# Attention with packed queries and a gated FFN on one core: the second batch's P run scored with the first units, its weights turned through DRAM, and the steps listed anew

## The chip, the cores and the metric

The kernel runs on one core of a Trainium2 chip. The metric is device time in microseconds (us). The core has TensorE (PE for its matmuls, PEld for its weight loads), VectorE (DVE), ScalarE (ACT), GpSimd (POOL) and SyncE (SP), which here issues nearly all DMA transfers. Each engine has its own queue and works through it in order.

## The reference

Eight batches of eight heads, 576 tokens, head dimension 64. Thirty-two packed queries P attend to the tokens of their batch and head, then the tokens attend to what the packed queries gathered, and a gated feed-forward net runs over all 4608 tokens:

```
def sm_attn(qq, kk, vv):
    s = scale * np.matmul(qq, kk.transpose(0, 1, 3, 2))
    s = s - np.max(s, axis=-1, keepdims=True)
    a = np.exp(s)
    a = a / (np.sum(a, axis=-1, keepdims=True) + 1e-09)
    return np.matmul(a, vv)
p_packed = sm_attn(p, k, v)              # (8, 8, 32, 64)
out = sm_attn(q, p_packed, p_packed)     # (8, 8, 576, 64)
x = out.transpose(0, 2, 1, 3).reshape(4608, 512)
h = x @ w_in                             # w_in 512 x 2048
g = h * (1.0 / (1.0 + np.exp(-1.702 * h)))
result = g @ w_out                       # w_out 2048 x 512
```

All inputs and the output are float32.

## The kernel before

The work is done batch by batch, with the attention of the next batch woven into the FFN of the present one. The heads of a batch are held as two groups, eo = 0 and 1, of four heads with 32 packed queries each: 128 partitions.

**The P run of a batch.** `scores1_mm` (L278, its matmuls in L250) multiplies P with the keys, a half (288 tokens) at a time and both groups together, into two PSUM banks. `scores1_copy` (L289) copies a bank into an SBUF tile x of 576 columns; `scores1_max` (L293, the reduction is L295) takes the maximum of one bank, so that there are four per batch; `bias1` (L299) joins the two maxima of a group and scales them. `exp1` (L317) makes the weights. These must be turned, since the tokens are the contraction of the next product. There are two ways to do it. By TensorE: `turn1_mm` (L339, matmul L343, four transposes into a bank), `turn1_copy` (L345), and for the last 64 tokens `turn1_last_mm` (L351, matmul L354) and `turn1_last_copy` (L358), which puts them into the tile aT. By VectorE and DRAM: `turn1_blocks` (L372, L374) transposes every 32x32 block of a group, eight `turn1_out` (L376, L382) per batch write the blocks to the DRAM tile aside, and six `turn1_in` (L384, L394) read them in another order into aT. Batches 0 and 1 go by TensorE, batches 2 to 7 by DRAM. `pack` (L396, matmul L406) multiplies with v; `pack_end` and the `pack_turn` steps make PT, the transposed packed values.

**The token run.** `scores2_mm` (matmul L493) multiplies q with PT, `scores2_turn` (L504) is a block transpose by DVE out of PSUM, `max2` (L524), `sub2` (L528), `exp2` (L532), `sum2` (L537 to L539) and `norm2` (L543) are the softmax, `turn2` (L549) turns back. `a_upper` and `a_lower` split its result into two parts ahi and alo of lower precision, whose sum is the value.

**The FFN.** `m_chunk` (L435) multiplies PT with a 512-wide part of w_in, so the attention's second product and the first FFN product become one: `h_mm` (matmul L603) is six matmuls of 288 columns from the split halves. A step `m_chunk b, fc` makes the factors of four units of h (a unit is 128 of the 2048 columns), and `m_upper` and `m_lower` (L469) split them. `h_tanh` (L611) and `h_gate` (L593) are the gate, `h_upper` (through `move`, L117 on ACT and L119 on DVE) and `h_lower` (L590) split g into ghi and glo, and `out_mm` is three matmuls of 512 columns (L663) that add a unit to one of four token tiles in PSUM. `store` (L682) writes a finished token tile. What a batch has beyond four token tiles of 128 is collected in over tiles.

**The FFN weights** come in as 64-bit words. `load_w n` (L189) loads one of 32 pieces, `begin_w` (L208, ACT) and `join_w` (L220, DVE) make float32 of it, and for w_out `upper_w` (a `move`) and `lower_w` (L232, POOL unless told otherwise) split it. Weights 4 to 7, 12 to 15, 20 to 23 and 28 to 31 are the four rows of w_out pieces that the units 0 to 15 of out_mm need, all in batch 0, where they arrive just ahead of use; the others are w_in.

**What sets the order.** A tuple `order` in the kernel (L707 to L1399) lists 2860 steps, and a loop (L1400) runs them. An instruction is put on its engine's queue where its step stands in the list. In `order`, `inner` names the two banks of h_mm (psh), `bank_b` the two banks used by m_chunk and pack (psb), `early` and `late` the four banks of out_mm. The x tiles have five buffers; a step that needs a new one waits for the oldest to be read. An engine's name at the end of a step (`dve`, `pool`) says where it runs.

Of the kernel before, what the change touches and what calls it, by code (L numbers as in the profile page):

```python
# [8 lines left out]
F32 = mybir.dt.float32  # L9
# [6 lines left out]
ALU = mybir.AluOpType  # L16
AX = mybir.AxisListType
# [4 lines left out]
def kernel(  # L22
# [77 lines left out]
    def x_tile(name):  # L100
        return wk.tile([P, S], F32, tag="x", name=name, bufs=5)
# [191 lines left out]
    def scores1_max(b, half, eo):  # L293
        bank = st["bank", 1, b, half][eo]
        nc.vector.tensor_reduce(  # L295
            st["mx", 1, b, eo][:, half : half + 1], bank[:, :NH], axis=AX.X, op=ALU.max
        )
# [399 lines left out]
    def over_store(pair, k, engine=nc.sync):  # L697
# [10 lines left out]
        (load, "k", 0, 0), (scores1_first, 0), (load, "k", 0, 1), (max1_first, 1, 0),  # L708
        (max1_first, 0, 0), (scores1_first, 1), (warm, 7, 3), (max1_first, 0, 1), (bias1, 0, 0),
        (exp1_first, 0, 0), (exp1_first, 0, 1), (turn1_mm, 0, 0), (max1_first, 1, 1),  # L710
        (bias1, 0, 1), (exp1_first, 1, 0), (exp1_first, 1, 1), (load_w, 1, 0), (sum1, 0, 0),
        (warm, 4, 2), (load, "v", 0, 0), (turn1_copy, 0, 0, dve), (turn1_mm, 0, 1),
        (turn1_last_mm, 0), (sum1, 0, 1), (load, "v", 0, 1), (turn1_last_copy, 0, dve),
        (pack, 0, 0, late), (turn1_copy, 0, 1), (pack, 0, 1), (begin_w, 1, 0), (join_w, 1, 0),
        (pack_end, 0), (load_w, 2, 0), (begin_w, 2, 0), (warm, 5, 2), (join_w, 2, 0),
        (pack_turn_mm, 0), (pack_turn_copy, 0), (load, "q", 0, 0), (scores2_mm, 0, 0),
        (scores2_turn, 0, 0, 0), (max2, 0, 0, 0), (scores2_turn, 0, 0, 1), (max2, 0, 0, 1),
        (sub2, 0, 0, 0, pool), (warm, 0, 3), (load_w, 3, 0), (begin_w, 3, 0), (warm, 8, 3),
        (warm, 9, 3), (load_w, 0, 0), (begin_w, 0, 0), (join_w, 3, 0), (exp2, 0, 0, 0),
        (join_w, 0, 0), (sum2, 0, 0, 0), (norm2, 0, 0, 0, pool), (load, "q", 0, 1),  # L720
        (scores2_mm, 0, 1, late), (scores2_turn, 0, 1, 0), (scores2_turn, 0, 1, 1), (max2, 0, 1),
        (load_w, 3, 1), (warm, 10, 3), (load_w, 4), (begin_w, 3, 1), (join_w, 3, 1),
        (m_chunk, 0, 0, early, 0), (turn2, 0, 0, 0), (m_upper, 0, 0, 0, 0), (m_upper, 0, 0, 1, 0),
        (sub2, 0, 0, 1, pool), (warm, 6, 2), (exp2, 0, 0, 1), (sum2, 0, 0, 1), (begin_w, 4),
        (join_w, 4), (a_upper, 0, 0, 0), (a_lower_mm, 0, 0, 0, bank_b), (sub2, 0, 1, None, pool),
        (exp2, 0, 1), (upper_w, 4), (a_lower_copy, 0, 0, 0), (load_w, 1, 1), (begin_w, 1, 1),
        (warm, 3, 3), (load_w, 0, 1), (sum2, 0, 1), (begin_w, 0, 1), (norm2, 0, 0, 1, pool),
        (turn2, 0, 0, 1), (load_w, 2, 1), (a_upper, 0, 0, 1), (m_lower, 0, 0, 0, 0), (warm, 2, 3),
        (begin_w, 2, 1), (m_lower, 0, 0, 1, 0), (join_w, 1, 1), (a_lower_mm, 0, 0, 1, bank_b),
        (a_lower_copy, 0, 0, 1), (h_mm, 0, 0, 0), (norm2, 0, 1, None, pool), (turn2, 0, 1),  # L730
        (lower_w, 4), (h_mm, 0, 1, 0), (h_tanh, 0, 0, 0), (a_upper, 0, 1, None), (a_lower, 0, 1),
        (h_tanh, 0, 1, 0), (join_w, 0, 1), (load_w, 5), (begin_w, 5), (join_w, 2, 1),
        (m_chunk, 0, 0, (bank_b, bank_b), 1), (load_w, 7), (begin_w, 7), (h_gate, 0, 0, 0),
        (h_upper, 0, 0, 0), (m_upper, 0, 0, 1, 1, dve), (h_mm, 0, 0, 1), (h_gate, 0, 1, 0),
        (h_upper, 0, 1, 0), (join_w, 5), (m_lower, 0, 0, 1, 1), (h_tanh, 0, 0, 1), (h_over, 0, 0),
        (h_gate, 0, 0, 1), (h_upper, 0, 0, 1, dve), (h_lower, 0, 0, 1, dve), (load_w, 6),
        (h_lower, 0, 0, 0), (h_mm, 0, 1, 1), (out_mm, 0, 0, 0), (upper_w, 5),
        (m_upper, 0, 0, 0, 1), (m_lower, 0, 0, 0, 1), (h_tanh, 0, 1, 1), (h_gate, 0, 1, 1),
        (out_mm, 0, 0, 1), (h_over, 0, 1), (out_mm, 0, 0, 3), (begin_w, 6), (join_w, 6),
        (load_w, 8), (begin_w, 8), (join_w, 8), (h_lower, 0, 1, 0), (h_mm, 0, 2, 1),  # L740
        (h_tanh, 0, 2, 1), (h_over, 0, 2), (load_w, 9), (lower_w, 5), (out_mm, 0, 1, 0),
        (h_upper, 0, 1, 1), (begin_w, 9), (load_w, 10), (begin_w, 10), (h_mm, 0, 2, 0),
        (h_tanh, 0, 2, 0), (join_w, 7), (join_w, 9), (out_mm, 0, 0, 2), (h_lower, 0, 1, 1),
        (out_mm, 0, 1, 3), (out_mm, 0, 1, 2), (load_w, 11), (h_gate, 0, 2, 1), (h_gate, 0, 2, 0),
        (begin_w, 11), (join_w, 11), (out_mm, 0, 1, 1), (upper_w, 6), (join_w, 10),
        (load, "k", 1, 0), (scores1_mm, 1, 0, inner), (load, "k", 1, 1), (scores1_max, 1, 0, 0),
        (h_upper, 0, 2, 0), (h_upper, 0, 2, 1), (h_lower, 0, 2, 0, dve), (scores1_copy, 1, 0, 0),
        (upper_w, 7), (scores1_max, 1, 0, 1), (m_chunk, 0, 1), (m_upper, 0, 1, 0, None, dve),
        (scores1_copy, 1, 0, 1), (load_w, 12), (begin_w, 12), (h_lower, 0, 2, 1), (h_mm, 0, 3, 0),
        (h_tanh, 0, 3, 0), (lower_w, 6), (h_mm, 0, 3, 1), (m_lower, 0, 1, 0), (out_mm, 0, 2, 2),  # L750
        (m_upper, 0, 1, 1, None), (h_gate, 0, 3, 0), (join_w, 12), (out_mm, 0, 2, 1), (lower_w, 7),
        (m_lower, 0, 1, 1), (h_upper, 0, 3, 0), (upper_w, 12), (lower_w, 12), (out_mm, 0, 2, 3),
        (load_w, 18), (h_lower, 0, 3, 0), (h_tanh, 0, 3, 1), (h_gate, 0, 3, 1), (h_over, 0, 3),
        (h_mm, 0, 4, 0), (h_tanh, 0, 4, 0), (h_gate, 0, 4, 0), (h_upper, 0, 4, 0),
        (h_upper, 0, 3, 1), (h_lower, 0, 3, 1), (out_mm, 0, 2, 0), (h_mm, 0, 4, 1),
        (h_tanh, 0, 4, 1), (out_mm, 0, 3, 0), (h_over, 0, 4), (h_gate, 0, 4, 1),
        (h_upper, 0, 4, 1, dve), (h_lower, 0, 4, 1, dve), (h_mm, 0, 5, 1), (load_w, 13),
        (begin_w, 13), (join_w, 13), (load_w, 14), (begin_w, 14), (join_w, 14), (out_mm, 0, 3, 2),
        (h_tanh, 0, 5, 1), (h_mm, 0, 5, 0), (h_over, 0, 5), (h_gate, 0, 5, 1), (h_lower, 0, 4, 0),
        (out_mm, 0, 4, 0), (out_mm, 0, 3, 1), (load_w, 15), (begin_w, 15), (upper_w, 13),  # L760
        (lower_w, 13), (h_tanh, 0, 5, 0), (h_gate, 0, 5, 0), (load_w, 17), (begin_w, 17),
        (join_w, 17), (h_upper, 0, 5, 0), (out_mm, 0, 4, 1), (begin_w, 18),
        (scores1_mm, 1, 1, inner), (scores1_copy, 1, 1, 0), (scores1_max, 1, 1, 1),
        (scores1_copy, 1, 1, 1), (scores1_max, 1, 1, 0), (join_w, 18), (join_w, 15),
        (out_mm, 0, 3, 3), (out_mm, 0, 4, 3), (load, "v", 1, 0), (load_w, 16), (begin_w, 16),
        (join_w, 16), (upper_w, 14), (h_upper, 0, 5, 1), (h_lower, 0, 5, 1, dve), (h_mm, 0, 7, 0),
        (h_mm, 0, 6, 0), (h_tanh, 0, 7, 0), (bias1, 1, 0), (h_gate, 0, 7, 0), (h_tanh, 0, 6, 0),
        (h_gate, 0, 6, 0), (h_upper, 0, 6, 0, dve), (load_w, 19), (out_mm, 0, 4, 2), (begin_w, 19),
        (join_w, 19), (h_lower, 0, 5, 0), (out_mm, 0, 5, 2), (bias1, 1, 1),
        (h_upper, 0, 7, 0, dve), (h_lower, 0, 7, 0), (exp1, 1, 0), (sum1, 1, 0), (load_w, 21),  # L770
        (h_mm, 0, 7, 1), (h_tanh, 0, 7, 1), (h_gate, 0, 7, 1), (h_upper, 0, 7, 1, dve),
        (m_chunk, 0, 2), (h_over, 0, 7), (h_mm, 0, 6, 1), (upper_w, 15), (load_w, 27),
        (out_mm, 0, 5, 3), (m_upper, 0, 2, 1, None), (m_lower, 0, 2, 1), (m_upper, 0, 2, 0, None),
# [667 lines left out]
```

## Time and profile before

| what | value |
|---|---|
| median of 3 runs | 702.9 us (702.71 to 703.27) |
| time of the profiled execution | 703.17 us |
| its span in the profile | 701.4 us |
| granted TensorE clock | 0.999 |
| ACT busy | 260.4 us (37%), 622 instructions |
| DMA | 64.01 MB, mean 91 GB/s |

The span is what the profile sees of the execution; the execution's own time is 1.8 us longer. The profile page gives busy time by engine, the span in 40 slices, the DMA queues, the chain of work that ended last (followed back from the last instruction, at each step to what released it), and groups of instructions by source line. A timeline lists single instructions; in square brackets at the end of a row stand the engine's idle time before it and what ended that. Such a row begins with its start and its length, both in us.

The slices show where the engines other than TensorE are loaded, and DMA with them (each digit is a tenth of busy time in 17.5 us):

```profile
DVE  4978885536655376654465558765685657855453
ACT  4778644423324323533322333332222332333220
POOL 1654343022502223111242220000000000000000
...
DMA  9788303250210711046000442035200060010001
```

### The profile page before, as it was taken

The page shows a single profiled execution, that of the slowest core. Times are in us where ns is not written, and L with a number is a line of the kernel's source. Part 1 is how long each engine was busy: PE and PEld are TensorE (multiplying, and loading weights), DVE is VectorE, ACT ScalarE, POOL GpSimd, SP SyncE. Part 2 cuts the span into 40 slices and gives each one's busy share as a digit, 9 for nine tenths or more (in the row PEclk, how much of TensorE's full clock was granted, in tenths as well). Part 3 has the DMA queues.
Part 4 walks back from the last instruction along what each step waited for, and adds up shares of the span by engine and source line. Part 5 has one row for each costly group of instructions (what it writes and reads, how often), then busy time and mean ns, then how long its engine had stood idle before and what let it go on. Part 6 is the DMA issues. An engine that isn't in the chain of part 4 may idle for free.

```text
span 701.4 us, 13028 instructions
## 1 busy us (share of the span) xinstructions
PE 685.9 (98%) x5032; PEld 559.9 (80%) x5032; DVE 437.9 (62%) x1093; ACT 260.4 (37%) x622; POOL 125.5 (18%) x146
## 2 busy tenths in 40 slices
PE   6899999999999999999999999999999999999997
PEld 4678788878888787887887888888888887888885
DVE  4978885536655376654465558765685657855453
ACT  4778644423324323533322333332222332333220
POOL 1654343022502223111242220000000000000000
PEclk9999999999999999999999999999999999999999
DMA  9788303250210711046000442035200060010001
GB/s 340 312 297 349 129 0 139 39 166 1 91 41 15 229 41 67 1 117 211 1 16 16 109 144 76 16 79 155 80 31 1 4 192 2 1 61 1 1 11 65
DMA packets 49853, 64.01 MB, mean 91 GB/s; under 512 B 30976, under 2 KB 35456, under 8 KB 48768
## 3 DMA queue, kind: packets, MB, share of 16 engines
q1 hardware_dynamic: 49712, 63.05, 27.6%
q8 instruction: 40, 0.66, 0.4%
q14 instruction: 21, 0.17, 0.1%
q10 hardware_dynamic: 80, 0.13, 0.0%
HBM read 50.19 MB, written 12.98 MB: 90 GB/s over the span
## 4 chain that ended last, share of the span: by engine, by line
PE 91%; DVE 4%; DMA 2%; issue 1%; SPq 1%; ACT 1%; DVEq 0%; ACTq 0%
PE acc L663 48%; PE h L603 28%; PE acc_over L663 5%; PE psm_None L435 4%; PE pspv L406 1%; PE ps L250 1%; PE ps L493 1%; PE warm L125 1%; DMA k<-pk 1%; DVE glo L590 1%; DMA aside<-xb 1%; DVE mlo L469 0%; DVE wo L232 0%; DMA aT<-aside 0%; SPq L382 0%
## 5 line engine op out<-in xcount | busy, mean ns | idle before, releaser
L663 PE MATMUL acc<-wo,ghi 128*128 128x512 f32 x1024 | 322.9, 396 | 0.0
L663 PEld LDWEIGHTS acc<-wo,ghi 128*128 128x128 f32 x1024 | 179.7, 188 | 39.7 <-issue 11.2
L611 ACT ACTIVATE g<-h 128x288 f32<-128x288 f32 x256 | 104.0, 411 | 283.4 <-PE h L603 268.7
L663 PE MATMUL acc<-wo,glo 128*128 128x512 f32 x512 | 202.1, 395 | 1.2 <-DVE glo L590 1.2
L593 DVE SCALAR_TENSOR_TENSOR g<-g,h 128x224 f32<-128x224 f32 (+1 forms) x256 | 105.3, 416 | 121.2 <-ACT g L611 120.2
L603 PE MATMUL h<-ahi,mhi 128*128 128x288 f32 x496 | 140.4, 298 | 1.7 <-DVE g L593 0.9
L603 PE MATMUL h<-ahi,mlo 128*128 128x288 f32 x496 | 138.8, 295 | 0.0
L663 PEld LDWEIGHTS acc<-wo,glo 128*128 128x128 f32 x512 | 96.1, 188 | 24.9 <-DVE glo L590 2.4
L590 POOL TENSOR_TENSOR glo<-g,ghi 128x288 fp32r<-128x288 f32 (+1 forms) x93 | 71.7, 779 | 236.4 <-ACT ghi L117 117.6
L603 PEld LDWEIGHTS h<-ahi,mhi 128*128 128x128 f32 x496 | 93.2, 188 | 19.2 <-DVE x L504 5.7
L603 PE MATMUL h<-alo,mhi 128*128 128x288 f32 x496 | 105.1, 293 | 0.0
L603 PEld LDWEIGHTS h<-ahi,mlo 128*128 128x128 f32 x496 | 93.4, 188 | 7.0
L590 DVE TENSOR_TENSOR glo<-g,ghi 128x224 fp32r<-128x224 f32 (+1 forms) x163 | 74.0, 467 | 19.8 <-ACT ghi L117 16.3
L603 PEld LDWEIGHTS h<-alo,mhi 128*128 128x128 f32 x496 | 79.7, 188 | 0.3 <-POOL alo L572 0.2
L117 ACT CAST ghi<-g 128x224 fp32r<-128x224 f32 (+1 forms) x134 | 52.7, 405 | 46.5 <-DVE g L593 37.3
L593 DVE SCALAR_TENSOR_TENSOR over<-g,h 128x64 f32<-128x64 f32 x128 | 27.6, 216 | 35.1 <-ACT g L611 34.8
L119 DVE CAST ghi<-g 128x224 fp32r<-128x224 f32 (+1 forms) x122 | 37.8, 317 | 7.0 <-PE acc L663 1.4
L469 DVE TENSOR_TENSOR mlo<-psm_None,mhi 128x512 fp32r<-128x512 f32 x60 | 40.7, 684 | 2.0 <-ACT mhi L117 1.7
L663 PE MATMUL acc_over<-wo,ghi_over 128*128 128x512 f32 x128 | 39.8, 392 | 0.0
L117 ACT CAST mhi<-psm_None 128x512 fp32r<-128x512 f32 x42 | 24.4, 586 | 23.9 <-PE psm_None L435 23.8
L435 PE MATMUL psm_None<-w_in,PT 64*32 64x512 f32 x496 | 33.2, 596 | 0.0
L663 PEld LDWEIGHTS acc_over<-wo,ghi_over 128*128 128x128 f32 x128 | 23.6, 188 | 4.7
(95 smaller groups left out, 493.7 us busy)
## 6 DMA issues: line engine op xcount, KB each, us to landing
q<-q SPq DMA_DIRECT2D x16, 576.0 KB, 6.0
v<-v SPq DMA_DIRECT2D x8, 1024.0 KB, 5.7
o<-o SPq DMA_DIRECT2D x32, 256.0 KB, 2.4
raw<-w_out SPq DMA_DIRECT2D x16, 511.8 KB, 6.2
raw<-w_in SPq DMA_DIRECT2D x12, 511.8 KB, 7.8
k<-pk SPq DMA_DIRECT2D x8, 640.0 KB, 4.2
k<-pk SPq DMA_DIRECT2D x8, 576.0 KB, 5.5
aside<-xb SPq DMA_DIRECT2D x48, 72.0 KB, 2.3
```

Source lines behind the costliest of these rows:

```text
L117: nc.scalar.copy(dst, src)
L119: engine.tensor_copy(dst, src)
L125: nc.tensor.matmul(t[:, :P], ident, ident, start=True, stop=True)
L250: nc.tensor.matmul(bank[32 * j : 32 * j + 32, :NH], kq["p", b][rows(eo), j, :], kq["k", b][rows(eo), half, j, :], start=True, stop=True,)
L406: nc.tensor.matmul(bank[32 * j : 32 * j + 32, e * D : (e + 1) * D], aT[:, c, e, 32 * j : 32 * j + 32], vt[:, c, e0 : e0 + D], start=(c == ...
L435: nc.tensor.matmul(banks[eo][32 * j : 32 * j + 32, columns(part)], PT[rows(eo), j, :], w_in_sb[fc][rows(eo), j, columns(part)], start=True ...
L469: nc.vector.tensor_tensor(lo, bank[:, at], hi.bitcast(F32), op=ALU.subtract)
L590: engine.tensor_tensor(lo, src, hi.bitcast(F32), op=ALU.subtract)
L593: nc.vector.scalar_tensor_tensor(dst, th, 1.0, h, op0=ALU.add, op1=ALU.mult)
L603: nc.tensor.matmul(h[:, :NH], m[eo][part][:, fo : fo + P], a[:, eo * NH : (eo + 1) * NH], start=(n == 0), stop=(n == len(terms) - 1),)
L611: nc.scalar.activation(g, st["h", b, f, half][:, :NH], AF.Tanh, scale=1.702)
L663: nc.tensor.matmul(acc, gp[:, at : at + P], wo[f][:, part, :], start=(start and i == 0), stop=(stop and i == 2),)
```

## The change

There are four parts. The x tiles get a sixth buffer. `scores1_max` takes one maximum per group, from the 576-wide copy x in SBUF and no longer from the two banks; it therefore stands behind both `scores1_copy` steps. `bias1` only scales for the batches after the first (batch 0, which takes its maxima in `max1_first`, joins two as before). And the steps are listed anew, from the first step to about nine tenths of the list; the last 284 steps are the same.

```
     def x_tile(name):
-        return wk.tile([P, S], F32, tag="x", name=name, bufs=5)
+        return wk.tile([P, S], F32, tag="x", name=name, bufs=6)
...
-    def scores1_max(b, half, eo):
-        bank = st["bank", 1, b, half][eo]
+    def scores1_max(b, eo):
         nc.vector.tensor_reduce(
-            st["mx", 1, b, eo][:, half : half + 1], bank[:, :NH], axis=AX.X, op=ALU.max
+            st["mx", 1, b, eo][:, 0:1], st["x", 1, b, eo], axis=AX.X, op=ALU.max
         )
...
-        nc.vector.tensor_scalar(nb, mx[:, 0:1], mx[:, 1:2], -SCALE, op0=ALU.max, op1=ALU.mult)
+        if b == 0:
+            nc.vector.tensor_scalar(nb, mx[:, 0:1], mx[:, 1:2], -SCALE, op0=ALU.max, op1=ALU.mult)
+        else:
+            nc.vector.tensor_scalar(nb, mx[:, 0:1], -SCALE, None, op0=ALU.mult)
...
-        (scores1_mm, 1, 1, inner), (scores1_copy, 1, 1, 0), (scores1_max, 1, 1, 1),
-        (scores1_copy, 1, 1, 1), (scores1_max, 1, 1, 0), (join_w, 18), (join_w, 15),
...
+        (scores1_mm, 1, 1, (bank_b, bank_b)), (scores1_copy, 1, 1, 0), (scores1_copy, 1, 1, 1),
+        (scores1_max, 1, 0), (h_mm, 0, 1, 0), (h_tanh, 0, 1, 0), (h_gate, 0, 1, 0),
```

In the new list, batch 1's scores of both halves stand with the first units of batch 0: the first half (`scores1_mm 1, 0`, in `inner`) ahead of the first `h_mm`, the second right behind it, in the banks of `bank_b`. Before, the first stood behind `out_mm 0, 1, 1` and the second between `out_mm 0, 4, 1` and `out_mm 0, 3, 3`. Batch 1's weights are no longer turned by `turn1_mm 1, 0`, `turn1_mm 1, 1` and `turn1_last_mm 1` with their three copies, but by two `turn1_blocks`, eight `turn1_out` and six `turn1_in`, as in the later batches. A number of steps of batches 0 to 3 go to another engine: POOL gets 115 instructions where it had 146. Lines behind L298 move down by up to two.

The rows below show, word for word, what stands in an engine's queue. Each names the line, the operation and what it writes and reads; a last number of a name tells buffers apart and differs between the two kernels.

First place: VectorE, between the two block transposes of batch 0's second scores (group 1) and its first `turn2` (tile xt). x2_0_0 and x2_0_1 are the scores of the two groups, mx2 and sm2 their maxima and sums, raw a loaded weight. Before:

```order
L504 STREAM_TRANSPOSE x2_0_1_278<-ps2_0_1_1_280 128x288
L524 TENSOR_REDUCE mx2_0_1_291<-x2_0_1_278 128x18
L220 SCALAR_TENSOR_TENSOR w_in0_79<-raw15_254,tops_83 128x256
L549 STREAM_TRANSPOSE xt_0_0_312<-x2_0_0_233 128x288
L537 TENSOR_REDUCE sm2_0_0_271<-x2_0_0_233 128x9
```

After:

```order
L506 STREAM_TRANSPOSE x2_0_1_262<-ps2_0_1_0_263 128x288
L526 TENSOR_REDUCE mx2_0_1_275<-x2_0_1_262 128x18
L220 SCALAR_TENSOR_TENSOR w_in0_79<-raw15_254,tops_83 128x256
L220 SCALAR_TENSOR_TENSOR w_in0_79<-raw13_277,tops_83 128x256
L539 TENSOR_REDUCE sm2_0_0_304<-x2_0_0_238 128x9
L540 TENSOR_SCALAR sm2_0_0_304<-sm2_0_0_304 128x9
L541 RECIPROCAL rs2_0_0_305<-sm2_0_0_304 128x9
L530 TENSOR_TENSOR x2_0_1_262<-x2_0_1_262,mx2_0_1_275 128x576
L539 TENSOR_REDUCE sm2_0_0_304<-x2_0_0_238 128x9
```

The subtraction of the second group (L530) is new on VectorE, where GpSimd had it, and one more join and the sums of both halves stand ahead of the first turn2, which follows eight rows further down.

Second place: SyncE in batch 0, where batch 1's v is loaded. raw tiles are weights, aside is the DRAM tile, xb the transposed blocks. Before:

```order
L189 DMA raw9_710<-w_in 128x2047
L151 DMA v_1_744<-v 128x2048
L189 DMA raw8_746<-w_in 128x2047
L189 DMA raw11_779<-w_in 128x2047
L189 DMA raw9_801<-w_out 128x2047
```

After:

```order
L189 DMA raw13_745<-w_in 128x2047
L384 DMA aside_1_748<-xb_1_0_733 576x1x32
L384 DMA aside_1_748<-xb_1_1_722 576x1x32 x2
L189 DMA raw9_878<-w_out 128x2047
L151 DMA v_1_887<-v 128x2048
L396 DMA aT_91<-aside_1_748 32x4x256
L189 DMA raw11_956<-w_out 128x2047
L189 DMA raw10_973<-w_out 128x2047
```

Five more writes to aside, like those shown, stand ahead of raw9. The writes and the reads stand among the loads, and v behind the writes.

Third place: the lower halves (L232) of the weights for the units 12 to 15, at the end of batch 0. wo12 to wo14 are the split weights; mlo_1 is batch 1's first m_chunk. VectorE before:

```order
L590 TENSOR_TENSOR glo_0_12_1205<-g_0_1_12_1215,ghi_0_12_1204 128x224
L232 TENSOR_TENSOR wo12_1156<-dec_1153,wo12_1156 128x512
L232 TENSOR_TENSOR wo14_1250<-dec_1202,wo14_1250 128x512
L469 TENSOR_TENSOR mlo_1_0_1_1295<-psm_1_0_1_None_1226,mhi_1_0_1_1294 128x512
L593 SCALAR_TENSOR_TENSOR g_0_0_13_1306<-g_0_0_13_1306,h_0_0_13_1260 128x288
```

GpSimd after:

```order
L592 TENSOR_TENSOR glo_0_12_1223<-g_0_1_12_1207,ghi_0_12_1222 128x224
L232 TENSOR_TENSOR wo12_1217<-dec_1191,wo12_1217 128x512
L592 TENSOR_TENSOR glo_0_13_1281<-g_0_0_13_1277,ghi_0_13_1280 128x288
L530 TENSOR_TENSOR x2_1_1_1247<-x2_1_1_1247,mx2_1_1_1262 128x576
L545 TENSOR_TENSOR x2_1_0_1088<-x2_1_0_1088,rs2_1_0_1288 128x576
L232 TENSOR_TENSOR wo14_1211<-dec_1209,wo14_1211 128x512
```

Both halves stood back to back on VectorE, ahead of the gate of unit 13 (L593), and are now on GpSimd, with a split, a subtraction and a norm between them.

More of the change, by code (lines that the diff above doesn't have):

```diff
@@ L714 @@
[L714 to L737, printed above, removed]
@@ L744 @@
[L744 to L749, printed above, removed]
@@ L768 @@
[L768 to L773, printed above, removed]
```

1090 lines of the change are left out of this document (564 added, 526 removed).

## The prediction

> **What bounds the kernel now.** I read four views: busy time by engine, the chain of waits that ended last, busy time by stretch, and TensorE's timeline, where I looked for steps longer than their like.
>
> ```profile
> span 701.4 us, 13028 instructions
> PE 685.9 (98%) x5032; PEld 559.9 (80%) x5032; DVE 437.9 (62%) x1093; ACT 260.4 (37%) x622; POOL 125.5 (18%) x146
> ...
> PE 91%; DVE 4%; DMA 2%; issue 1%; SPq 1%; ACT 1%; DVEq 0%; ACTq 0%
> ```
>
> TensorE is busy for 685.9 of 701.4 us and makes up 91% of the chain. So the end moves only where TensorE gets fewer matmuls or waits less, and 15.5 us is all the idle time there is.
>
> ```profile
> 0.00:20.00 20.00, 14.22 (x213) 9.34 (x213) 9.92 (x29) 8.21 (x24) 4.81 (x16) 1.00 0.92 349
> 20.00:40.00 20.00, 17.91 (x132) 13.00 (x132) 18.66 (x41) 15.62 (x36) 12.71 (x12) 1.00 0.79 303
> 45.00:60.00 15.00, 15.00 (x108) 11.79 (x107) 12.52 (x33) 12.58 (x27) 7.01 (x9) 1.00 0.82 311
> 60.00:75.00 15.00, 15.00 (x179) 12.61 (x185) 13.00 (x24) 13.05 (x28) 8.46 (x8) 1.00 0.56 227
> ```
>
> The columns are stretch, length, busy time of PE, PEld, DVE, ACT and POOL, granted clock, DMA share and GB/s. In the first 40 us TensorE lacks 5.78 + 2.09 = 7.9 us, half of its idle time. From 20 to 40 us DVE is busy for 18.66 of 20: that stretch is DVE's. Behind 45 us TensorE is full, and what is lost is single waits.
>
> **The change, part by part. Turn matmuls of batch 1 (removed).**
>
> ```profile
> 59.98 0.60 PE L343 MATMUL pst<-ident,x 128*128 128x128 f32 x4
> 60.33 0.38 PE L603 MATMUL h<-ahi,mhi 128*128 128x288 f32 x1
> ...
> 66.91 0.60 PE L343 MATMUL pst<-ident,x 128*128 128x128 f32 x4
> 67.27 0.71 PE L663 MATMUL acc<-wo,ghi 128*128 128x512 f32 x2
> ...
> 68.85 0.38 PE L354 MATMUL pstl<-ident,x 128*128 128x128 f32 x2
> 68.98 0.71 PE L663 MATMUL acc<-wo,ghi 128*128 128x512 f32 x2
> ```
>
> Ends are modelled, so I count from start to start: 0.35 + 0.36 + 0.13 = 0.84 us. TensorE is full there, so it comes off the time: **-0.8**.
>
> **Waits of before that go.** Ordinary steps first, five pieces of the chain in a row, and a bank:
>
> ```profile
> 277.26 0.80 PE h L603 x6
> 278.05 0.70 PE acc L663 x3
> 278.75 1.02 PE psm_None L435 x16
> 279.77 0.59 PE ps L250 x16
> 280.36 0.45 DVE mx L295
> ...
> 280.84 0.41 ACT x L117
> ```
>
> So an h_mm costs 0.8 us, an out_mm 0.7, of which one matmul is 0.23, an m_chunk 1.0, a scores step 0.6. The distances below are from the start of the last matmul ahead of a wait to the start of the next.
>
> ```profile
> 90.46 3.21 DVE L232 TENSOR_TENSOR wo<-dec,wo 128x512 fp32r<-128x512 f32 x2
> ...
> 93.38 0.40 PE L663 MATMUL acc<-wo,glo 128*128 128x512 f32 x1
> 94.69 0.40 PE L603 MATMUL h<-ahi,mhi 128*128 128x288 f32 x1 [0.91 <-DVE g L593]
> ...
> 235.78 0.40 PE L663 MATMUL acc<-wo,glo 128*128 128x512 f32 x1
> 237.35 0.26 PE L406 MATMUL pspv<-v,aT 128*32 128x64 f32 x4 [1.17 <-DMA aT<-aside]
> ...
> 273.60 0.40 PE L663 MATMUL acc<-wo,ghi 128*128 128x512 f32 x1
> 274.55 0.50 PE L663 MATMUL acc<-wo,glo 128*128 128x512 f32 x1 [0.55 <-DVE glo L590]
> ...
> 280.76 0.40 PE L663 MATMUL acc<-wo,glo 128*128 128x512 f32 x1
> 281.29 0.40 PE L603 MATMUL h<-ahi,mhi 128*128 128x288 f32 x1
> ```
>
> By the order each releaser now stands elsewhere. At 94.69 the gate waits behind two lower halves of weights on DVE; now both are POOL's. Distance 1.31 less 0.23: 1.1 us. At 237.35 batch 3's pack waits for its weights from DRAM: 1.57 less 0.23 is 1.3. The list had 15 out_mm, 6 h_mm and one scores step between the last scores and this pack, and now has 17, 7 and 1: two out_mm of 0.7 and an h_mm of 0.8 are 2.2 us more cover for a lack of 1.3. At 274.55 a split waits behind a norm2 on DVE, which the new list moves: 0.95 less 0.23 is 0.7. At 281.29 (0.53 less 0.23: 0.3) the bank of the scores is late: in the chain above the copy (L117) starts only when the maximum over the bank (L295) is done. With the maximum taken from the copy, the bank is free 0.45 us sooner. Sum of the four: 1.1 + 1.3 + 0.7 + 0.3 = **-3.4**. Bounds: 0 if other late work is right behind each, -3.4 if nothing is.
>
> **The start.**
>
> ```profile
> 24.07 0.69 DVE L220 SCALAR_TENSOR_TENSOR w_in<-raw,tops 128x256 uint32<-128x256 uint32 x1
> ...
> 24.28 0.29 PE L603 MATMUL h<-ahi,mhi 128*128 128x288 f32 x1
> ...
> 31.70 0.50 PE L663 MATMUL acc<-wo,glo 128*128 128x512 f32 x1 [0.65 <-DVE glo L590]
> ...
> 40.30 0.40 PE L603 MATMUL h<-ahi,mhi 128*128 128x288 f32 x1 [0.33 <-ACT x L117]
> L528 DVE TENSOR_TENSOR x<-x,mx 128x576 f32<-128x576 f32 x9 | 7.9, 879 | 0.2
> ```
>
> Ahead of the first turn2, DVE gets one more join_w (0.69) and sub2 of batch 0's second group of heads (0.88), which POOL had; some of this falls into DVE's waits. My hand-laid order of DVE puts the first h_mm at 25.7 to 26.2, which is 1.4 to 1.9 later than 24.28. Back come: batch 1's first scores step, done ahead of it (0.6 us); the wait at 31.70 (0.65), since TensorE now comes there later than its split; the wait for a bank at 40.30 (0.3). That is 1.55, so even. What comes new is m_chunk 0,1, which now stands where a weight's join, one of a run of joins on DVE, is still to come: 0.6 to 1.3 us. I take **+0.7** for the start; bounds -0.8 (all given back, no new wait) and +2.2 (sub2 and a join run beside POOL's and stretch).
>
> For how far they stretch, the row is 90.46: 1.6 us for each of two DVE instructions beside POOL ones, where 0.88 is the mean of a like one above. The Trainium skill (SBUF — State Buffer, section "Who interferes with whom") says that a VectorE instruction with two SBUF inputs and a GpSimd one that reads SBUF lock each other out for the whole instruction. By that rule sub2 would wait out a POOL instruction and the start would come to the upper bound; by the mean of the row it stays at the lower. The trace agrees in kind: 1.6 against 0.88.
>
> **Batch 1's weights by DRAM.** TensorE's 0.84 us become two DVE transposes, 8 writes and 6 reads on SP's queue, and the copies out of PSUM go.
>
> ```profile
> 131.00:139.00 8.00, 8.00 (x47) 7.09 (x46) 4.98 (x15) 3.66 (x10) 1.57 (x2) 1.00 0.48 75
> L374 DVE STREAM_TRANSPOSE xb<-x 128x576 f32<-128x576 f32 x12 | 9.1, 771 | 5.1 <-ACT x L319 5.0
> v<-v SPq DMA_DIRECT2D x8, 1024.0 KB, 5.7
> ...
> raw<-w_in SPq DMA_DIRECT2D x12, 511.8 KB, 7.8
> ...
> aside<-xb SPq DMA_DIRECT2D x48, 72.0 KB, 2.3
> aT<-aside SPq DMA_DIRECT2D x24, 128.0 KB, 2.6
> ```
>
> DVE: 2 x 0.77 us, beside matmuls. DMA: batch 2's eight writes are alone from 131 to 139 us, 0.48 x 8 = 3.8 us of all DMA engines for 0.6 MB. Free from 45 to 75 us are 15 x 0.18 + 15 x 0.44 = 9.3 us, so it fits, but weights, q and v come later by up to 4 us. Time of the path: the scores' second step follows the first h_mm at about 27.5; the list has 34 out_mm, 20 h_mm, 3 m_chunk and a scores step from there to pack 1, which is 34 x 0.7 + 20 x 0.8 + 3 x 1.0 + 0.6 = 43 us, so the pack is due at 70.5 to 71.5. The writes stand behind the transposes at 51 to 52.5 and are through at about 58. Then SP issues three weights (0.5 MB each), v (1 MB) and the six reads (0.6 MB): 3.1 MB at 311 GB/s is 10 us, and 2.6 for landing would end at 70.6; the reads are not all last, so some 1 to 3 us remain. I cost it at nothing; the cover is the 43 us. If it fails, see the third rival.
>
> The Trainium skill (DMA: Bandwidth & Descriptors, section "Specifications") gives 512 B as the least transfer for full rate, and the turned weights are written in runs of 128 B. That speaks against the change. The rows agree: 72 KB take 2.3 us where 128 KB, read back in longer runs, take 2.6. By that rule alone the writes would crowd the loads out, and the time would be the third rival's.
>
> **Maxima from the copy.** 28 reductions become 14 of twice the length:
>
> ```profile
> L295 DVE TENSOR_REDUCE mx<-ps 128x1 f32<-128x288 f32 x28 | 12.1, 450 | 10.3 <-PE ps L250 9.2 <-ACT x L117 1.2
> ```
>
> At 0.45 us to 0.9 us each (no longer to twice as long) the 14 take 6.3 to 12.6 us where 28 took 12.1; DVE works beside matmuls there, so neither counts. But the maximum now comes behind both copies, which makes the path from scores to exp up to 0.9 us longer; from batch 2 on it has its cover, as worked out for batch 3. The sixth x buffer issues nothing and costs nothing.
>
> **New waits.** Halves, splits and norms change engines in the list up to 610 us. Laying the rows' durations along the list, I find: m_chunk 0,2 waits for a join (0.35 to 1.0), the lower half of weight 28, now on POOL, ends just after out_mm wants it (0.3), that of 31 too (0.4), and the handing over to batch 3's h_mm is tight (0.4). With 0.2 for what I don't see: **+1.9**; bounds 0 and +4, a little more than what the old list lost.
>
> **Sum.** Against the profiled execution's own 703.17: -0.8 - 3.4 + 0.7 + 1.9 = -1.6, so 701.5. That execution lies 0.3 above the median of 702.9, so the measured median should be **701.2**.
>
> **The rivals.** (1) The new list has no waits of its own behind 45 us: -0.8 - 3.4 + 0.7 = -3.5, and 699.4; with the start at its lower bound 697.9. For: the list before had only four such waits in 650 us. Against: it was as tight and had four. (2) The start keeps what the rest gains: DVE is the bound there (18.66 of 20), first h_mm at 27 or later, +2.2 for +0.7: 702.7. (3) Slower: pack 1 waits for DRAM. Place: SP's queue and the DMA engines from 51 to 72 us, with weights ahead of the reads. At the 227 GB/s that the next stretch moved, 3.1 MB take 13.7 us, and the reads land at 58 + 13.7 + 2.6 = 74.3, some 3.3 us behind the pack; batch 1's m_chunk and scores come late with it. 701.2 + 3.3 = 704.5, with another weight late 706. It decides if the last read lands behind about 71.5. For: batch 3 waited 1.17 us on that very transfer. Against: the 43 us of cover, twice batch 3's. (4) The list names other waits but the same ones come back, since TensorE meets a late DVE wherever it is: only 0.8 goes, 702.1.
>
> **How the numbers follow.** Forecast 0.48 (699.9 to 702.3), (1) 0.17, (2) 0.12, (3) 0.15, (4) 0.08. The range reaches from rival 1 with its start to near the first value of (3): 698.0 to 704.8. A measurement here tells 0.2%, 1.4 us, from no change: faster is below 701.5, slower above 704.3. Faster: 0.32 of the forecast's 0.48 and all of (1), 0.49. Slower: (3) and a little of (2), 0.17. Same: 0.34.
>
> **What would show it.** In the profile after: first h_mm at 25.5 to 26.5 (behind 27: rival 2); no turn matmul after 15 us; no wait above 0.5 us on TensorE at 94, 235 and 274; pack 1 without a wait for aT from aside, or with one of more than 1 us (rival 3); DMA share from 45 to 75 us at 0.8 or above; TensorE's busy time down by about 1 us. I am wrong if the start is off by over 1.5 us either way, or if new waits add up to more than 4 us.

## The result and the profile after

| | before | changed |
|---|---|---|
| median, first comparison | 703.02 us (702.71 to 703.27, 4 runs) | 698.5 us (697.16 to 698.87, 4 runs) |
| ratio, 95% interval | | 0.9925 [0.9913, 0.9936] |
| three later comparisons | 703.25, 703.03, 703.23 us | 699.3, 698.05, 698.07 us |
| their ratios | | 0.9950 [0.9932, 0.9967], 0.9924 [0.9912, 0.9937], 0.9928 [0.9915, 0.9942] |
| profiled execution | 703.17 us, span 701.4 | 697.16 us, span 695.4 |

The kernel is 4.0 to 5.2 us faster; 1.7 were forecast. In all four sets the profiled execution of the changed kernel was the fastest of its set, by up to 1.5 us under the median. So its waits are a lower bound, and beside the 6.0 us by which the first two profiled executions differ stand 4.0 to 5.2 between medians.

The page of the profile after, first lines and chain:

```profile
span 695.4 us, 12968 instructions
PE 685.3 (99%) x5022; PEld 561.1 (81%) x5022; DVE 439.1 (63%) x1111; ACT 258.1 (37%) x620; POOL 96.1 (14%) x115
...
PE 93%; DMA 3%; DVE 1%; issue 1%; SPq 1%; ACT 0%; DVEq 0%; ACTq 0%
```

TensorE's busy time is down by 0.6 us and the span by 6.0: what went is waiting. DVE's share of the chain fell from 4% to 1%; DMA's rose from 2% to 3%. The view that says it at a glance groups TensorE's waits by what ended them (total, times, longest). Before:

```profile
PE psal L564 <- DVE xt L549: 1.3, 2, 0.7
PE acc L663 <- DVE glo L590: 1.2, 2, 0.6
PE pspv L406 <- DMA aT<-aside: 1.2, 1, 1.2
PE h L603 <- DVE g L593: 0.9, 1, 0.9
PE h L603 <- ACT x L117: 0.7, 3, 0.3
```

After (the whole answer but for the wait for the first keys, which was 5.2 us and is 1.9, since six warm-up matmuls now run ahead of them):

```profile
PE warm L125 <- POOL ident masks.py:199: 1.4, 1, 1.4
PE warm L125 <- ACT x L117: 0.5, 1, 0.5
PE psm L437 <- DVE w_in L220: 0.5, 1, 0.5
PE pspt L427 <- ACT pn L421: 0.4, 1, 0.4
PE h L605 <- DVE g L595: 0.3, 1, 0.3
```

Of the five waits of before, 5.3 us together, one of 0.3 us is left; the others named after are at the start, ahead of the first h_mm. The stretches, in the order of the prediction:

```profile
0.00:20.00 20.00, 15.75 (x212) 10.43 (x213) 10.25 (x30) 7.90 (x22) 4.26 (x15) 1.00 0.91 345
20.00:40.00 20.00, 19.35 (x159) 14.63 (x158) 18.53 (x46) 17.57 (x41) 11.51 (x11) 1.00 0.86 330
45.00:60.00 15.00, 15.00 (x93) 12.32 (x92) 12.23 (x26) 11.59 (x25) 8.36 (x9) 1.00 0.83 245
60.00:75.00 15.00, 14.95 (x171) 12.38 (x176) 12.76 (x29) 9.01 (x21) 4.90 (x5) 1.00 0.93 279
```

TensorE lacks 4.25 + 0.65 = 4.9 us in the first 40, where it lacked 7.9. Of these 3.0 us, 1.4 are no gain: the same 54 warm-up matmuls (`warm`), moved about and run sooner, are 9.8 us long in sum where they were 8.4. Counting steps is safer. At 40.30 the old kernel had done 7 h_mm, 8 out_mm, 3 m_chunk steps and one scores step of batch 1; at 39.90 the changed one has done one h_mm (0.8) and one scores step (0.6) more, so it is 1.8 us ahead. DVE is as full as it was from 20 to 40 us (18.53 for 18.66), so DVE did not get less to do; TensorE got work, the scores, that does not wait for it. From 60 to 75 us the DMA share is 0.93 where it was 0.56. Single rows at the places of the prediction:

```profile
19.51 0.70 DVE L530 TENSOR_TENSOR x<-x,mx 128x576 f32<-128x576 f32 x1
20.95 0.84 PE L250 MATMUL ps<-k 64*32 64x288 f32 x16
24.72 0.29 PE L605 MATMUL h<-ahi,mhi 128*128 128x288 f32 x1
44.69 0.40 PE L605 MATMUL h<-ahi,mhi 128*128 128x288 f32 x1 [0.28 <-DVE g L595]
```

The first h_mm is at 24.72, 0.4 us later than before and 1.0 to 1.5 earlier than forecast, with batch 1's first scores step already done at 20.95.

### The profile page after: what moved, and what is told of

The parts are those of the page before. It is cut to its first block, busy times and chain, and to the rows that moved or that the text cites. A ratio compares the mean times of both kernels' runs of the same rounds, so it can differ in the third digit from the quotient of the medians.

```text
span 695.4 us, 12968 instructions
## 1 busy us (share of the span) xinstructions
PE 685.3 (99%) x5022; PEld 561.1 (81%) x5022; DVE 439.1 (63%) x1111; ACT 258.1 (37%) x620; POOL 96.1 (14%) x115
## 2 busy tenths in 40 slices
DMA packets 55260, 65.18 MB, mean 94 GB/s; under 512 B 35808, under 2 KB 40864, under 8 KB 54176
## 3 DMA queue, kind: packets, MB, share of 16 engines
q1 hardware_dynamic: 55120, 64.23, 29.2%
## 4 chain that ended last, share of the span: by engine, by line
PE 93%; DMA 3%; DVE 1%; issue 1%; SPq 1%; ACT 0%; DVEq 0%; ACTq 0%
PE acc L665 50%; PE h L605 28%; PE acc_over L665 5%; PE psm_None L437 4%; DMA aT<-aside 2%; PE pspv L408 1%; PE ps L250 1%; PE ps L495 1%; DMA k<-pk 1%; PE warm L125 1%; SPq L384 1%; DMA aside<-xb 0%; DVE ghi L119 0%; DVE x L506 0%; PE pst L345 0%
## 5 line engine op out<-in xcount | busy, mean ns | idle before, releaser
L595 DVE SCALAR_TENSOR_TENSOR g<-g,h 128x288 f32<-128x288 f32 (+1 forms) x256 | 104.9, 415 | 116.4 <-ACT g L613 115.8
L592 DVE TENSOR_TENSOR glo<-g,ghi 128x224 fp32r<-128x224 f32 (+1 forms) x183 | 76.1, 427 | 14.8 <-ACT ghi L117 10.8
L592 POOL TENSOR_TENSOR glo<-g,ghi 128x224 fp32r<-128x224 f32 (+1 forms) x73 | 55.5, 767 | 191.3 <-DVE ghi L119 88.1
L117 ACT CAST ghi<-g 128x288 fp32r<-128x288 f32 (+1 forms) x142 | 55.2, 403 | 54.4 <-DVE g L595 47.6
L119 DVE CAST ghi<-g 128x224 fp32r<-128x224 f32 (+1 forms) x114 | 35.9, 320 | 7.0 <-PE acc L665 1.4
L117 ACT CAST mhi<-psm_None 128x512 fp32r<-128x512 f32 x45 | 26.2, 584 | 29.3 <-PE psm_None L437 29.3
```

The costliest lines, as they stand in the source:

```text
L117: nc.scalar.copy(dst, src)
L119: engine.tensor_copy(dst, src)
L592: engine.tensor_tensor(lo, src, hi.bitcast(F32), op=ALU.subtract)
L595: nc.vector.scalar_tensor_tensor(dst, th, 1.0, h, op0=ALU.add, op1=ALU.mult)
```

## The experiments

Every list named old or new is that of before or of the change. Times are medians, ratios against before on the same chip.

**1. The change again** (no edit). 

> The changed kernel once more, unchanged. Theory: it runs 4.3 to 5.0 us below before (698.0 to 698.7), and what its executions differ by (697.2 to 698.9 so far, where before's differ by 0.6) is the wait of batch 1's pack for the reads of aT: in the profile the pack waits 0.2 us in an execution of 697.2 and 1 to 1.7 us in one near 698.5. Rival: they differ at the start (the first h_mm between 24.7 and 26 us), and the pack waits the same 0.2 us in all.

699.3 us, 0.9950 [0.9932, 0.9967]. In this profile the pack waits 0.5 us for the reads, with the first h_mm at 24.68, as in the first one. The profiled execution was again the fastest of its set (697.83), so what the slower ones wait for was not seen here. Other runs speak for the rival, that executions differ at the start. In the four profiles of the change the first pack begins at 11.1 to 11.5 us. In runs 2, 9 and 10, with the same steps up to there, it begins at 12.3 to 12.8, and these three profiled executions were 1.0 to 1.4 us slower than the medians of their sets. But run 6's second profile has it at 12.4 in an execution of median length, so this is not shown to be the whole spread.

**2. New start, old rest.** The new list's first steps up to h_mm 0,5,0, then whatever the old list has left, in its order, with TensorE's turn and the maxima from the copy.

```
+ order = new[: end of (h_mm, 0, 5, 0)] + [s for s in old if s not yet done]
```

> The new list up to h_mm 0,5,0 (about 45 us), then the old one, with batch 1 turned by TensorE as before and every maximum taken from the copy. Theory (the start gained, which the prediction had at +0.7): -1.7 for the start and -0.3 to -0.6 for the maxima, so 2.0 to 2.3 us below before. Rival (the prediction's own sum was right at the start, and the surplus is in the later list): 0 to +0.7, so the time of before or a little above.

704.96 us, 1.0024 [1.0016, 1.0033]: slower than before, so it met neither number. The reason is in the fourth run: the old list with the maxima from the copy, which is the base to compare with, is at 706.9. Against that base the start brings 1.9 us, about what the theory had for it (1.7). This is a difference of medians; the two profiled executions, run 2's the slowest of its 12 and the base's the fastest of its six, do not show it.

**3. Old start, new rest.** The same the other way round.

```
+ order = old[: end of (h_mm, 0, 5, 1)] + [s for s in new if s not yet done]
```

> The old list up to h_mm 0,5,1 (about 46 us), then the new one, with batch 1's second scores directly behind the joint, its weights turned through DRAM and maxima from the copy. Theory: the three late waits (-3.2), the bank (-0.4) and the turn matmuls (-0.8) are gone, which is -4.4; but the second scores come 24 us later than in the new list and the weights by DRAM are late for the pack, so of this 3 to 8 us are given back there: 2 us below to 4 above before, and with the wait at the pack taken out 4 below. Rival (the late list brings nothing without the new start): no late wait is gone, and it is at least as slow as before beside the pack's wait.

703.13 us, 1.0002 [0.9989, 1.0014]. At the joint it waits for splits and weights that one list has already put off and the other not yet done. TensorE's timeline there:

```profile
55.15 0.49 PE L665 MATMUL acc<-wo,ghi 128*128 128x512 f32 x1 [0.43 <-POOL wo L232]
56.35 0.51 PE L665 MATMUL acc<-wo,glo 128*128 128x512 f32 x1 [0.71 <-POOL glo L592]
57.48 0.37 PE L605 MATMUL h<-ahi,mhi 128*128 128x288 f32 x1 [0.62 <-DVE g L595]
```

Behind 76 us it has no wait above 0.2 us at all: the late waits go with the new rest, whatever the start. In run 2 they are there, one of them here:

```profile
94.57 0.40 PE L605 MATMUL h<-ahi,mhi 128*128 128x288 f32 x1 [0.90 <-DVE g L595]
```

**4. Old list, maxima from the copy.**

```
- (scores1_max, b, 0, eo), (scores1_max, b, 1, eo)
+ (scores1_max, b, eo)     # behind both copies of eo; bias1 behind it
```

> The old list, with one thing changed: the maximum of each group is taken from the copy, behind its two copies (and six x buffers). Theory: the banks come free 0.45 us sooner, and the waits at 38.9, 40.3, 281.3 and 386 go: 0.6 to 1.2 us below before; the waits at 94, 235 and 274 stay. Rival (the maxima carry the later gains as well): 3 us or more below before. Other rival (the longer path from scores to exp costs as much): no change, with the pack of batch 3 waiting longer than 1.2 us.

706.9 us, 1.0050 [1.0037, 1.0062]: 3.6 us slower, where all three readings had it faster or equal. TensorE's waits for gates in it, then one of them with the row of VectorE that causes it:

```profile
PE h L605 <- DVE g L595: 2.7, 4, 0.9
```

```profile
226.87 0.78 DVE L376 STREAM_TRANSPOSE xb<-x 128x576 f32<-128x576 f32 x1 [1.00 <-ACT x L321]
```

```profile
228.18 0.40 PE L605 MATMUL h<-ahi,mhi 128*128 128x288 f32 x1 [0.66 <-DVE g L595]
```

The waits for banks (`h <- ACT x`, 0.7 us before) are gone, as the mechanism has it. But the maximum now comes behind both copies, exp behind it, and VectorE stands for 1.00 us at the block transpose with two gates queued behind it, for which an h_mm then waits. In before that transpose began at 224.75 after 0.31 us. Of the four waits the longest, 0.90 at 94.60, is before's own; new are those at 228, 396 and 564 us.

**5. Maxima from the banks in the new list** (the reverse).

```
- (scores1_max, b, eo)
+ (scores1_max, b, half, eo)     # directly behind (scores1_copy, b, half, eo)
```

> The changed kernel with the old form of the maxima: one for each bank, directly behind that bank's copy in the list, joined in bias1. Theory (alone in the old list the new form cost 3.6 us, because a list made for one form has the other in the wrong places): 1 to 3 us above the changed kernel, from banks that come free 0.45 us later. Rival (the old form is the better one wherever it stands, and the new list gained in spite of the new one): 1 us or more below the changed kernel.

703.67 us, 1.0006 [0.9995, 1.0016]: all of the gain is lost. The largest wait is at the start, where batch 1's early scores now hold their banks until VectorE has taken the maxima; a stretch behind it shows the granted clock (the number ahead of the last two):

```profile
23.43 1.15 PE L125 MATMUL warm<-ident 128*128 128x128 f32 x6 [1.85 <-DVE mx L295]
24.00:26.00 2.00, 2.00 (x8) 1.63 (x7) 1.34 (x4) 0.48 (x2) 0.00 (x0) 0.50 1.02 405
```

The first h_mm is at 26.78, 2.1 us later than in the change, and its matmuls are slow: the clock is 0.50 from 24 to 26 us and 0.64 from 26 to 28, where the change has 1.00. The first matmul of h_mm 0,3,0 is at 41.03 for 38.31. So 2.7 of the 6.15 us between the two profiled executions are lost by then, in part to the clock. A later wait, VectorE's row and then TensorE's:

```profile
206.14 0.45 DVE L295 TENSOR_REDUCE mx<-ps 128x1 f32<-128x288 f32 x1
```

```profile
206.65 0.40 PE L603 MATMUL h<-ahi,mhi 128*128 128x288 f32 x1 [0.77 <-DVE mx L295]
```

The bank comes free with the maximum. Runs 4 and 5 together: neither form is the better by itself; each costs 3.6 us or more in a list that was laid out for the other, though close to half of what run 5 lost comes from the one place at the start.

**6. TensorE's turn in the new list.**

```
- (turn1_blocks, 1, eo), (turn1_out, 1, eo, j), (turn1_in, 1, i)
+ (turn1_mm, 1, 0), (turn1_copy, 1, 0)          # at h_mm 0,8,0
+ (turn1_mm, 1, 1), (turn1_copy, 1, 1)          # at h_mm 0,9,0
+ (turn1_last_mm, 1), (turn1_last_copy, 1)      # at out_mm 0,8,0
```

> The changed kernel with one part undone: batch 1's weights are turned by TensorE again (three turn matmul steps, three copies), the eight writes and six reads are gone. Theory: the matmuls come back (+0.8), the pack's wait for the reads goes (0.2 to 0.7 by the two profiles so far, and some waits for weights behind it): within 0.5 us of the changed kernel's 699.3. Rival (the DRAM path is wholly covered and the turn a clean gain, as the prediction had it): 0.8 to 1.0 us above the changed kernel. Other rival (the DMA traffic is what makes the changed kernel's times spread): below it by 0.5 or more, with a spread like before's.

697.89 us, 0.9922 [0.9908, 0.9936]. It lies below run 1 (0.9950), but not in one comparison with it, so it was done again beside the changed kernel. 

> The changed kernel unchanged, on one chip with the next run, for a direct comparison. Theory and rival both: 698.3 to 699.5.

 

> The changed kernel with batch 1's weights turned by TensorE again, a second time. Theory (the DRAM path gives back what its matmuls save and more, by the pack's wait and by weights that come late): 697.5 to 698.3, and 0.5 to 1.4 us below the changed kernel on the same chip. Rival (the difference seen was between chips): the same as the changed kernel within 0.5.

698.05 us (0.9924) for the change and 698.41 (0.9926 [0.9914, 0.9939]) with TensorE's turn: the same. As it is listed here the DRAM turn brings nothing. TensorE's share of the chain is 96% in run 6, and no wait for aT is in it. The stretches from 45 to 75 us of run 6, to be held against those of the change above:

```profile
45.00:60.00 15.00, 14.97 (x91) 12.33 (x92) 10.76 (x22) 11.45 (x27) 8.20 (x9) 1.00 0.66 247
60.00:75.00 15.00, 15.00 (x159) 12.88 (x158) 12.25 (x29) 10.80 (x25) 4.51 (x4) 1.00 0.57 217
```

With the DRAM turn the DMA engines are busy for 15 x 0.17 + 15 x 0.36 = 8 us more there, for 1.2 MB (the pages have 65.18 in all with it and 64.01 before).

**7. Reads first.** Batch 1's reads and the last of v ahead of the loads of weights 22 and 23.

```
- (load_w, 23), ..., (load_w, 22), (begin_w, 22), (turn1_in, 1, 2), ..., (turn1_in, 1, 4)
+ (turn1_in, 1, 2), ..., (turn1_in, 1, 4), (load_w, 23), (load_w, 22), ...
```

> The changed kernel with SyncE's order changed: the six reads of aT and the last part of v are issued ahead of the loads of weights 22 and 23, whose begin, join and split follow the pack. Theory (the pack waits because the reads share the DMA engines with weights issued ahead of them): the pack's wait goes, 0.3 to 0.7 us below the changed kernel, with weights 22 and 23 some 2 us later under a cover of 15. Rival (the reads are late by their own path, so the order on the queue doesn't matter): the wait stays, no change. Other rival: the weights become late, and out_mm 0,10 or 0,11 waits, 0.5 us or more above.

701.15 us, 0.9965 [0.9953, 0.9978]: the pack's wait goes, as the theory had it, and an out_mm waits for a weight, as the other rival had it:

```profile
75.72 0.50 PE L665 MATMUL acc<-wo,ghi 128*128 128x512 f32 x1 [1.03 <-DVE wo L119]
```

But the load is not what is late. By the landings in the trace the last read is there at 67.7, some 2.5 us sooner than in the change, and weight 23 at 69.25. Its begin stands behind pack_end in this edit, and ScalarE comes to it at 72.65 only. So the order on SyncE's queue does decide when the reads land. Whether the DRAM turn would pay with the reads first and the begins ahead of pack_end was not run.

**8. The subtraction on GpSimd.**

```
- (sub2, 0, 1, None)
+ (sub2, 0, 1, None, pool)
```

> The changed kernel with the subtraction of batch 0's second group back on GpSimd, at the same place of the list. Theory (in the changed kernel it took 0.70 us on VectorE while GpSimd was idle, and on GpSimd it takes 1.2 or more, with exp and sums behind it): the sums and so the first h_mm come 0.3 to 0.8 us later, time 0 to 0.8 us above the changed kernel. Rival (the prediction's: on VectorE it is a cost of 0.9 to 1.4 at the start): the first h_mm 0.7 us or more earlier and the time below by as much.

699.03 us, 0.9943 [0.9930, 0.9955]: 0.3 us below run 1 and 0.5 to 1.0 above the other three sets of the change, none of them in one comparison with it, so time alone does not settle it. In the profile the theory holds. GpSimd's row, and VectorE's, which stands for exp behind it:

```profile
20.73 1.16 POOL L530 TENSOR_TENSOR x<-x,mx 128x576 f32<-128x576 f32 x1
```

```profile
22.63 0.75 DVE L539 TENSOR_REDUCE sm<-x 128x18 f32<-128x576 f32 x1 [1.59 <-ACT x L534]
```

From the first scores2 matmul to the first h_mm it is 11.6 us (14.56 to 26.18), and 10.5 in the change (14.22 to 24.72): 1.1 us later, above the 0.3 to 0.8 expected.

**9. Lower halves on VectorE.**

```
- (lower_w, 28), (lower_w, 30)
+ (lower_w, 28, dve), (lower_w, 30, dve)
```

> The changed kernel with the lower halves of weights 28 and 30 on VectorE again, at their new places in the list. Theory (the wait at 94 us came from these two beside GpSimd's work, 1.1 us): a wait of 0.5 to 1.1 us is back on TensorE near 90 us, and the time is as much above. Rival (the new list has cover there whichever engine takes them, so the wait went by the places, not by the engine): no wait near 90 us, no change.

698.38 us, 0.9932 [0.9919, 0.9946], beside 698.05: no difference that can be measured, and no wait from 73 to 102 us. The rival holds: at the new places there is no wait whichever engine takes them. GpSimd at the old places was not run. Alone on VectorE the subtraction is short:

```profile
89.77 0.68 DVE L232 TENSOR_TENSOR wo<-dec,wo 128x512 fp32r<-128x512 f32 x1
```

It took 1.6 us at 90.46 before, beside GpSimd. The Trainium skill (SBUF — State Buffer, section "Who interferes with whom") has it that a VectorE instruction with two SBUF inputs and a GpSimd one that reads SBUF lock each other out; 0.68 alone and 1.6 beside agree with that.

**10. Batch 1's scores at their old places** (with TensorE's turn).

```
- (scores1_mm, 1, 0, inner)                  # ahead of h_mm 0,0,0
- (scores1_mm, 1, 1, (bank_b, bank_b))       # behind h_mm 0,0,0
+ (scores1_mm, 1, 0, inner)                  # behind out_mm 0,1,1
+ (scores1_mm, 1, 1, inner)                  # behind out_mm 0,4,1
```

> The changed kernel with TensorE's turn (as te_turn_2) and batch 1's scores back at their old places: behind out_mm 0,1,1 and behind out_mm 0,4,1, both in the banks of h_mm. Theory (scores in TensorE's idle time at the start are 0.6 us for nothing, and their banks cost waits of 0.3 to 0.6 us later): 1.0 to 2.0 us above te_turn_2, with the first h_mm about 0.3 us earlier. Rival (the start gained by the other moves on VectorE and GpSimd, not by the scores): within 0.5 us of te_turn_2.

699.91 us, 0.9955 [0.9943, 0.9968], beside 698.41: 1.5 us, as the theory had it, with the first h_mm 0.2 us earlier (25.39 for 25.59). The two steps themselves:

```profile
40.68 1.45 PE L250 MATMUL ps<-k 64*32 64x288 f32 x16
54.06 1.41 PE L250 MATMUL ps<-k 64*32 64x288 f32 x16
```

Each is 1.4 us long where an ordinary one takes 0.6, and in the old list the first took 0.5 at the same place (37.17 to 37.68 in before's timeline). So 1.5 us is what these places cost in the new list, in which other units hold the banks; it is not shown that the move saved as much.

**11. Where the DRAM turn gives back.** In the profile of the third run of the change (698.05 us) an h_mm waits 0.35 us at 65.22. The chain behind it:

```profile
55.46 5.33 DMA raw<-w_out
...
60.81 0.79 ACT tops L208
...
61.63 0.70 DVE dec L220
...
64.12 0.68 DVE wo L232
64.80 0.38 DVE g L595
...
65.22 1.07 PE h L605 x6
```

Weight 21 is issued at 55.46 behind the eight writes, its join and split stand ahead of a gate on VectorE, and the h_mm waits for the gate. The pack waits as well. So both were moved.

```
- (join_w, 21), (upper_w, 21, dve), ..., (lower_w, 21, dve), ..., (h_gate, 0, 8, 0)
+ (h_gate, 0, 8, 0), (join_w, 21), (upper_w, 21, dve), (lower_w, 21, dve)
...
- (pack, 1), (pack_end, 1), (load_w, 27), (begin_w, 27), (out_mm, 0, 8, 2)
+ (load_w, 27), (begin_w, 27), (out_mm, 0, 8, 2), (pack, 1), (pack_end, 1)
```

> The changed kernel, DRAM turn kept, with two places moved: VectorE's join and split of weight 21 stand behind the gate of unit 8 and no longer ahead of it, and batch 1's pack stands behind out_mm 0,8,2. Theory (the 0.8 us of the turn matmuls were given back there: 0.4 to 0.6 at the pack, which waits for the reads, and 0.4 to 0.5 at h_mm 0,9,0, whose gate stands behind weight 21, whose load comes behind the eight writes): both waits go, and the time is 0.5 to 1.0 us below the changed kernel. Rival (the waits turn up behind the next step, since batch 1's m_chunk and scores follow the pack directly): no change, with waits of the same size between 70 and 80 us.

 

> The changed kernel unchanged, on one chip with the run before, for a direct comparison: 698.0 to 699.3, with the two waits of 0.4 to 0.7 us at h_mm 0,9,0 and at the pack.

698.47 us (0.9930 [0.9916, 0.9944]) beside 698.07 (0.9928). The gate's wait is gone, but the edit put ScalarE's wait for weight 27 ahead of pack_end, and the pack's turn waits 1.25 us for it. So once more, with `(pack_end, 1)` ahead of `(load_w, 27), (begin_w, 27)`: 

> As cover_moved, but ScalarE's begin of weight 27, which waits for its load, stands behind pack_end; in cover_moved it came to stand ahead of it, and the pack's turn waited 1.25 us for it. Theory (the turn's saving was given back at the gate of unit 8 and at the pack): neither wait is left above 0.3 us, the pack's turn is on time, and the time is 0.5 to 1.0 us below the changed kernel's 698.1, that is 697.1 to 697.6. Rival (what is saved there is lost behind it): 698.0 to 698.5, with waits of 0.5 us or more between 72 and 90 us.

698.23 us, 0.9928 [0.9914, 0.9941]: the rival. TensorE comes to the pack earlier and waits there, by its timeline and the chain:

```profile
71.63 1.32 PE L408 MATMUL pspv<-v,aT 128*32 128x64 f32 x80 [0.55 <-DMA aT<-aside]
```

```profile
61.59 9.68 DMA aT<-aside
71.28 0.35 issue
71.63 1.25 PE pspv L408 x72
```

A read issued at 61.59 lands at 71.28. What TensorE saves ahead of it, the pack waits, and the pack's turn behind it waits 0.52 us more at 73.47.

No version was measurably faster than the changed kernel; runs 6, 9 and 11 equal it.

## Why the prediction came out too small

**The start** was the step that failed most: +0.7 forecast, about -1.9 measured (run 2 against run 4; 1.8 by the count of steps at 40 us). In the rows of the change: the first h_mm 0.4 us later, less 0.6 for a scores step done ahead of it, and of the waits behind it (0.65 at 31.70, 0.3 at 40.30, and more below 0.5 us each) one of 0.28 is left. Three parts were mis-sized. The subtraction on VectorE was priced as a cost of 0.9 to 1.6 us; it took 0.70, and on GpSimd it costs 1.1 us at the first h_mm (run 8). Run 8's expectation has GpSimd idle beside it, and it was not: a norm began there, and GpSimd paid.

```profile
19.74 1.00 POOL L545 TENSOR_TENSOR x<-x,rs 128x288 f32<-128x288 f32 x1 [2.08 <-DVE rs L541]
21.17 0.67 POOL L545 TENSOR_TENSOR x<-x,rs 128x288 f32<-128x288 f32 x1 [0.43 <-DVE rs L541]
```

The first norm ran beside the subtraction (19.51 to 20.21) and took 0.33 us more than the second of its shape, beside a reduction. So the two did meet, but the one that had begun first lost nothing; the forecast's upper bound had VectorE as the loser. The early scores were priced at 0.6 plus 0.3; undone in the new list they cost 1.5 (run 10), so the price was not too high, and how the 1.9 divide between them and the other moves stays open. And the new wait of m_chunk 0,1 (0.6 to 1.3) did not come: the one row of that kind (`psm <- w_in`, 0.5 us) stands at 18.83, ahead of the first h_mm.

**Late waits that go**, -3.4: right in sum. The waits of 0.9, 1.2 and 0.6 us at 94, 237 and 274 are gone from the change and from run 3, and there in run 2 (0.90, 0.95 and 0.53); from 90 to 610 us TensorE's idle time fell from 2.9 us to nothing. For the wait at 94 the reason was not needed: the new places do without GpSimd (run 9).

**New waits**, +1.9: the four named (m_chunk 0,2, weights 28 and 31, batch 3's start) did not come. In their place stand two at the DRAM turn, at h_mm 0,9,0 and at the pack: by the distance between matmuls less an ordinary step 0.2 us together in the first profile and 0.6 to 1.1 in the three later ones. So this term was off by 0.8 to 1.7.

**The turn**, -0.8: the matmuls went (5032 to 5022), the time did not (run 6). The forecast had the path arrive 1 to 3 us ahead of the pack at 70.5 to 71.5. The pack's place was nearly right, at 70.15; the arrival was not. The sum had put it at 70.6 if the reads came last, and took 1 to 3 us off because they do not; a read landed at 70.13. It had a landing at the 2.6 us of an ordinary read. The chain of the change shows what it is with the engines at 0.93:

```profile
57.33 6.88 DMA aT<-aside
...
64.23 5.90 DMA aT<-aside
...
70.15 1.32 PE pspv L408 x80
```

So the third rival's mechanism was there, at the price of what the turn saved and no more. The Trainium skill (DMA: Bandwidth & Descriptors, section "Specifications") has 512 B as the least transfer for full rate. The trace agrees: from 45 to 60 us the writes of 128 B runs put the share from 0.66 (run 6) to 0.83 while the bytes stay at 247 and 245 GB/s.

**Maxima from the copy**, at nothing: wrong both ways round. Alone they cost 3.6 us, and taking them out of the new list costs 4.4 to 5.6 (703.67 against 699.3 and 698.1), 2.7 of it at the start by the profile of run 5. "From batch 2 on it has its cover" was the sentence that failed: the cover is the order of the list, and the old one has none.

**The sum** by the measured sizes is -0.8 - 3.4 - 1.9 + 0.2 = -5.9 for the first profiled execution, which was 6.0 us faster, and -5.0 with the 1.1 of the second. That it comes so close is in part luck, since the 1.9 are taken from medians of two other lists. The medians, 4.0 to 5.2, fall short of the second figure by up to 1.0; later first packs, as under run 1, are a likely part of that and not shown to be all. The result is where the first rival had it with its start at the lower bound, 697.9 to 699.4.

## What to carry to other kernels

An instruction moved to a busy engine is not a cost by its length alone: ask what waits for it where it stood, and whether its old engine was slower or queued. An edit to a step's form can't be priced apart from the order in which it is issued: the same edit was worth 4.4 to 5.6 us in one order and cost 3.6 in another. And a transfer's landing has to be taken from a stretch as loaded as the one that it moves into.

## What the runs showed of the hardware

SyncE's queue seems to hold eight transfers at a time. In the change, the read issued at 64.23 was 0.02 us behind the landing of the one issued at 57.33, the eighth before it (the chain quoted last), and the issues at 63.38 and 65.20 stand 0.01 us behind the landings of the eighth before them (63.37 and 65.19). With landings of 6 to 9 us that makes the queue's order a matter of its own.

The start of one list varied: the first h_mm of the same steps stood at 24.68 us in run 1 and at 26.07 in run 2, since the first pack began at 11.4 in one and at 12.8 in the other. TensorE was slow for longer in run 2: the two turns of four matmuls ahead of the pack took 0.97 and 0.64 us in run 1 and 1.17 and 1.06 in run 2, and the clock records of the traces begin full speed at 9.7 and at 13.3 us.

And one wait cost clock. In run 5 TensorE stood for 1.85 us up to 23.43, and its granted clock was 0.50 from 24 to 26 us and back at 1.00 by 28. A wait of 1.25 us at the same place in run 10 was not followed by a loss (1.00 from 20 to 28 us).
